# Attention plus gated MLP on one core: one q/k block transpose moved behind the next block's PV work, sums put in another order

## The chip, the core and the metric

One Trainium2 chip, one of its cores. The engines of a core run side by side, each through its own queue of instructions in order: TensorE (PE, matrix products; PEld is its weight load), VectorE (DVE), ScalarE (ACT), GpSimd (POOL) and SyncE (SP, which here only issues DMA transfers). The metric is device time in microseconds (us) for one launch of the whole kernel; less is better.

## The reference

Inputs are q, k, v of shape (8, 8, 576, 64) and the weights of an MLP. Attention is computed in separate chunks of 64 positions; its output, as 4608 rows of 512, goes through two matrix products with a swish between them.

```python
q_c = q.reshape(B, H, nc, chunk, D)            # k_c, v_c likewise, chunk = 64
scores = scale * np.matmul(q_c, k_c.transpose(0, 1, 2, 4, 3))
attn = np.exp(scores - np.max(scores, axis=-1, keepdims=True))
attn = attn / (np.sum(attn, axis=-1, keepdims=True) + 1e-09)
attn_out = np.matmul(attn, v_c)
...
x = attn_out.transpose(0, 2, 1, 3).reshape(B * S, H * D)   # 4608 x 512
h = x @ w_in                                               # 512 -> 2048
g = h * (1.0 / (1.0 + np.exp(-beta * h)))
return (g @ w_out).astype(np.float32)                      # 2048 -> 512
```

## The kernel before

The 4608 rows are nine blocks of 512 (`j` = 0 to 8, `NB` = 9). The order of all instructions is written out by hand: each engine runs its own in the order in which the Python code emits them. All matrix work is in fp16 with fp32 accumulation.

The loop over `j` = 1 to 8 (L675) works on two blocks at once: the MLP of block `j`, and, inside it, the attention of block `na = j + 1`, so that its input is there when the next turn begins.

**First product, `L1(j)` (L560).** x times w_in, partly by a seven-product (Strassen-Winograd) scheme: two `unit` calls make the hidden columns m = 0 to 7, and the plain products m = 8 to 15 (`emit_m`) stand between the unit's steps as spacers. A unit begins with the product `wA` on PE, which VectorE copies out of PSUM (`snap("u1")`, L319); the next product into the same bank (`wA<-xs,sw`) waits for this copy and for `xs`, the differences of x that `emit_xs` (L291 to L294) makes on VectorE. A unit has one sum on POOL (`t`, L342). `hooks` maps a number m to work that is emitted just ahead of `emit_m(j, m)`: loads of q, k, v, and block transposes. Block 1 alone goes through `L1_plain` (L540): there the first `nh` columns m are done in two halves of 256 rows, first halves first, since the last quarter of x still has to pass through a TensorE transpose (`emit_xp(7)`, in the hook -1) and a ScalarE copy (L235).

**Block transposes.** q and k of a batch arrive by DMA (`load_qk`, POOL queue); `T(b)` takes the next of batch b's four STREAM_TRANSPOSE instructions on VectorE (`emit_T`, L136; two halves of the heads, q and k each). Before the change `L1(j)` has all four of batch `j + 2` at the hooks 10, 13, 14 and 15. For `j` of 6 and more there is no batch `j + 2` left, and the hooks are empty.

**Sums.** The second product, g times w_out, uses the same seven-product scheme, and its operands are sums s1 to s4 of parts of g (`emit_sum(j, which, part)`, L373 for s3, L369 for s1, L371 for s2, L375 for s4), each in four parts p. Parts 0 and 2 of s3 are done on POOL, right after the units; all others on VectorE. s2 needs s1 of its part. The eight s1 and s2 sums are put on a list `fill` in the order p = 0, 2, 1, 3, and `dve(n)` emits the next n of them.

**Second product, `steps_L2(j)`.** Seven steps mm[0] to mm[6] on PE of 16 matmuls of 256 columns each. After mm[0], mm[2] and mm[4] ScalarE copies a bank out (u1, u2, u3, L422). After mm[2], POOL subtracts u1 and u2 (`w1`, printed as w, L449). `cB`, `cD` and `cC` are additions on VectorE (L430) whose results are stored, or kept as `t`.

**Attention of the next block.** `emit_sc` makes scores on PE and exponentials on ScalarE; `emit_pv(i, where)` makes 128 rows of x: 16 small matmuls into the PSUM bank `x` (where = "x") or into the two banks `sc0`, `sc1` (where = "s"), then on VectorE reciprocals (L210, L213) and products (L215), then a transposing DMA on SP's queue (L223) into `xt`. `pvs(n)` is the pair `emit_pv` n ("x") and n + 1 ("s"); the two pairs of a block, `pvs(0)` and `pvs(2)`, use the same banks, so PE can begin the second pair only when VectorE has read the first. `emit_xs(na)` waits for the four transposing DMAs.

So VectorE's order around the change is, for `j` from 2: unit 1, the hooks 13, 14, 15, s3 of parts 1 and 3, s1 and s2 of part 0 (`dve(2)`), `pvs(0)`, six sums (`dve(6)`), `pvs(2)`, four s4, cB, cD, xs, cC (`t`), and then the first copy (`u`) of the next unit.

Of the kernel before, what the change touches and what calls it, by code (L numbers as in the profile page):

```python
# [15 lines left out]
def kernel(  # L16
# [11 lines left out]
    B, H, S, D = q.shape  # L28
# [55 lines left out]
    def load_qk(b, split=False):  # L84
        for dst, nm in ((q_t, "qu"), (k_t, "ku")):
            dst[b] = qk_p.tile([128, 2, RUN, D], FP16, tag=nm, name=nm)
        for zs in ((slice(0, 1), slice(1, 2)) if split else (slice(0, 2),)):
            for src, dst in ((q, q_t), (k, k_t)):
                nc.gpsimd.dma_start(
                    out=dst[b][:, zs].rearrange("p z r d -> p z (r d)"),  # L90
                    in_=src[b].rearrange("(z a) (t r) d -> (a t) z (r d)", z=2, r=RUN)[:, zs],
                )
# [261 lines left out]
    def emit_m(j, m):  # L354
        emit_h(j, m)
        emit_g(j, m)
# [4 lines left out]
    def emit_sum(j, which, part):  # L361
        if j not in s_t:
            s_t[j] = [s_p.tile([128, NM, HT], FP16, tag=f"s{i}", name=f"s{i}") for i in range(4)]
        s1, s2, s3, s4 = s_t[j]
        g = gt_t[j]
        lo, hi = slice(2 * part, 2 * part + 2), slice(NM + 2 * part, NM + 2 * part + 2)
        tt = (nc.gpsimd if which == 3 and part in (0, 2) else nc.vector).tensor_tensor
        if which == 1:
            tt(out=s1[:, lo], in0=g[:, lo, dn], in1=g[:, hi, dn], op=ALU.add)  # L369
        elif which == 2:  # L370
            tt(out=s2[:, lo], in0=s1[:, lo], in1=g[:, lo, up], op=ALU.subtract)  # L371
        elif which == 3:
            tt(out=s3[:, lo], in0=g[:, lo, up], in1=g[:, lo, dn], op=ALU.subtract)  # L373
        else:
            tt(out=s4[:, lo], in0=g[:, hi, up], in1=s2[:, lo], op=ALU.subtract)  # L375
# [157 lines left out]
    fill = []  # L533

    def dve(n=1):
        for _ in range(n):
            if fill:
                fill.pop(0)()
# [21 lines left out]
    def L1(j, hooks={}, first=None):  # L560
        gt_t[j] = gt_p.tile([128, KFF, BLK], FP16, tag="gt", name="gt")

        def sp(m):
            def f():
                hooks.get(m, lambda: None)()
                emit_m(j, m)
            return f

        if first:
            first()  # L570
        unit(j, 0, [sp(8), sp(9), sp(10)])
        unit(j, 1, [sp(11), sp(12), sp(13)])
        for p in (0, 2):
            emit_sum(j, 3, p)
        sp(14)()
        sp(15)()
        for p in (0, 2, 1, 3):
            fill.extend([lambda w=w, p=p: emit_sum(j, w, p) for w in (1, 2)])
        hooks.get(KFF, lambda: None)()

    def table(func):
# [2 lines left out]
    with tc.manual_schedule():  # L584
        load_qk(0, split=True)
        nc.vector.memset(zero, 0.0)
        nc.vector.memset(bstage, 0.0)
        nc.vector.memset(warm, 0.0)
        nc.scalar.activation(out=warm2, in_=warm, func=ACTF.Exp, scale=1.0)
        for g4 in range(4):  # L590
            nc.sync.dma_start(
                out=bstage[32 * g4:32 * g4 + NM].rearrange("p r i -> p (r i)"),
                in_=moe_beta.rearrange("(m g x) -> g m x", g=4, x=64)[g4],
            )
        for t in vbuf:
            nc.vector.memset(t[:, :, :, D:D + 1], 1.0)
        load_v(0)
        make_identity(nc, ident)
        for g in range(4):
            load_w_in(g)  # L600
        load_w_out(0)
        load_w_out(1)
        load_qk(1)
        load_w_out(2)
        load_v(1)
        load_w_out(3)
        load_qk(2)

        emit_idle(4)
        for f in T_items(0):  # L610
            f()
        nc.vector.transpose(
            out=bt, in_=bstage.rearrange("p r i -> p (r i)").rearrange("p (i r) -> p r i", r=2)
        )
        eps = 2.0 ** -10
        nc.vector.tensor_tensor(out=bm, in0=bt, in1=bt, op=ALU.mult)
        nc.vector.tensor_scalar(
            out=bm, in0=bm, scalar1=eps * eps, scalar2=None, op0=ALU.is_ge)
        nc.vector.scalar_tensor_tensor(
            out=beta2, in0=bt, scalar=eps, in1=bm, op0=ALU.subtract, op1=ALU.mult)  # L620
        nc.vector.tensor_scalar_add(beta2, beta2, eps)
        nc.vector.reciprocal(out=binv, in_=beta2)
        emit_sc(0, between=lambda: emit_idle(5))
        emit_sc(1, where="p")
        emit_idle(3)
        emit_pv(0, xbar=False)
        emit_pv(1, where="p", xbar=False)
        d = emit_idle(4, 256)
        emit_xp(0)
        emit_pv(2, xbar=False)  # L630
        emit_idle(2, d=d)
        emit_xp(1)
        emit_pv(3, where="p", xbar=False)
        emit_idle(3, d=d)

        L1_plain(0, {-2: lambda: emit_xp(2), -3: lambda: emit_xp(3)}, 4)
        emit_sw()
        scale_w_out(0)
        scale_w_out(1)
        emit_tw(1)  # L640
        T1 = T_items(1)
        T1[0]()
        T1[1]()
        T1[2]()
        T1[3]()
        scale_w_out(2, act=2)
        table(ACTF.Exp)
        load_v(2)
        load_qk(3)
        hooks = {  # L650
            8: lambda: [emit_sc(2, "x"), emit_sc(3)],
            10: lambda: [emit_pv(4, xbar=False), emit_pv(5, "s", xbar=False), scale_w_out(3, act=2)],
            12: lambda: [emit_pv(6, xbar=False), emit_xp(4), emit_xp(5)],
            14: lambda: [emit_pv(7, xbar=False), emit_xp(6)],
        }
        for kk, f in enumerate(L2_plain(0)):
            hooks.get(kk, lambda: None)()
            f()

        TQ = {b: T_items(b) for b in range(2, B)}  # L660

        def T(b, n=1):
            for _ in range(n):
                if TQ.get(b):
                    TQ[b].pop(0)()

        def loads(j):
            if j + 3 < B:
                load_qk(j + 3)

        def loads_v(j):
            if j + 2 < B:
                load_v(j + 2)

        for j in range(1, NB):  # L675
            na = j + 1
            late = j == 1
            if late:
                L1_plain(1, {
                    -1: lambda: [emit_xp(7), table(ACTF.Silu)], 3: lambda: emit_tw(3), 4: lambda: T(2), 5: lambda: T(2),  # L680
                    6: lambda: emit_tw(2), 7: lambda: T(2), 9: lambda: T(2),
                    10: lambda: emit_tw(4), 14: lambda: T(3), 15: lambda: T(3),
                    11: lambda: [loads(1), loads_v(1)],
                    KFF: lambda: [table(ACTF.Exp), emit_sc(4, "x"), emit_sc(5)],
                }, 2)
            else:
                L1(j, {8: lambda: loads(j), 10: lambda: T(j + 2), 11: lambda: loads_v(j),
                       13: lambda: T(j + 2), 14: lambda: T(j + 2), 15: lambda: T(j + 2)})

            def pv(n, where):  # L690
                if na < NB:
                    emit_pv(4 * na + n, where)

            mm, cB, cD, cC = steps_L2(j, last=(j == NB - 1))
            def pvs(n):
                pv(n, "x")
                pv(n + 1, "s")

            mm[0]()
            emit_sum(j, 3, 1)  # L700
            emit_sum(j, 3, 3)
            if late:
                dve(8)
                T(3, 2)
            else:
                dve(2)
                pvs(0)
            mm[1]()
            if late:
                pvs(0)  # L710
            dve(6)
            mm[2]()
            if not late:
                pvs(2)
            if na + 1 < NB and not late:
                table(ACTF.Exp)
            mm[3]()
            if late:
                pvs(2)
            for p in (0, 2, 1, 3):  # L720
                emit_sum(j, 4, p)
            cB()
            mm[4]()
            cD()
            if na + 1 < NB:
                emit_sc(2 * na + 2, "x")
                emit_sc(2 * na + 3)
            if na < NB:
                emit_xs(na)
            mm[5]()  # L730
            if j < NB - 1:
                cC()
            mm[6]()
            if na + 1 < NB:
                table(ACTF.Silu)
# [30 lines left out]
```

## Time and profile before

| what | value |
|---|---|
| device time, median of 4 runs | 279.87 us (279.78 to 280.16) |
| device time of the profiled execution | 280.9 us |
| its span, first to last instruction | 279.1 us |
| mean granted TensorE clock | 1.000 |
| PE busy | 263.2 us, 94% of the span |
| VectorE busy | 211.9 us, 76% |
| ScalarE busy | 163.5 us, 59% |
| POOL busy | 100.9 us, 36% |

The loop's turns in this execution, by the start of the first product of the next block on PE: j = 1 from about 51 us, then 81, 109.4, 138.1, 166.9, 195.3, 222.6 and 248.9 us. In a line of the timeline the first number is the start in us from the span's start, the second the length of the (merged) group, then engine, source line, operation, written tile <- read tiles, shape, count; what stands in brackets is idle time of the engine before it and what ended it. A VectorE instruction that does not wait can begin some 80 ns before the recorded end of the one in front.

### The profile page before, as it was taken

The page shows a single profiled execution, that of the slowest core. Times are in us where ns is not written, and L with a number is a line of the kernel's source. Part 1 is how long each engine was busy: PE and PEld are TensorE (multiplying, and loading weights), DVE is VectorE, ACT ScalarE, POOL GpSimd, SP SyncE. Part 2 cuts the span into 40 slices and gives each one's busy share as a digit, 9 for nine tenths or more (in the row PEclk, how much of TensorE's full clock was granted, in tenths as well). Part 3 has the DMA queues.
Part 4 walks back from the last instruction along what each step waited for, and adds up shares of the span by engine and source line. Part 5 has one row for each costly group of instructions (what it writes and reads, how often), then busy time and mean ns, then how long its engine had stood idle before and what let it go on. Part 6 is the DMA issues. An engine that isn't in the chain of part 4 may idle for free.

```text
span 279.1 us, 8198 instructions
## 1 busy us (share of the span) xinstructions
PE 263.2 (94%) x3509; PEld 188.2 (67%) x3509; DVE 211.9 (76%) x425; ACT 163.5 (59%) x276; POOL 100.9 (36%) x108
## 2 busy tenths in 40 slices
PE   2689999999999999999989999999999999998995
PEld 0355455547876687668866886688668866876684
DVE  2762755879668997899789978898759766977674
ACT  2149746879166836684568546853785478225820
POOL 8732343190108610871078104820342035203500
PEclk9999999999999999999999999999999999999999
DMA  6999999999677926792669442914201420241013
GB/s 100 175 207 210 211 181 207 218 231 186 77 141 139 155 41 137 137 172 42 115 136 178 57 101 92 86 41 109 83 0 40 117 75 0 41 138 53 2 38 114
DMA packets 69588, 31.99 MB, mean 115 GB/s; under 512 B 53680, under 2 KB 63920, under 8 KB 69552
## 3 DMA queue, kind: packets, MB, share of 16 engines
q0 software_dynamic: 44960, 18.35, 54.5%
q1 hardware_dynamic: 24448, 12.99, 18.5%
q8 instruction: 27, 0.44, 0.7%
q10 hardware_dynamic: 144, 0.13, 0.1%
q14 instruction: 9, 0.07, 0.1%
HBM read 36.71 MB, written 9.44 MB: 165 GB/s over the span
## 4 chain that ended last, share of the span: by engine, by line
PE 65%; DVE 19%; DMA 9%; issue 2%; ACT 2%; POOL 2%; DVEq 0%; ACTq 0%; POOLq 0%
PE hps L258 22%; PE oA L411 11%; PE wA L311 8%; DMA xt<-x 6%; PE wX L311 5%; PE ops L510 5%; DVE x L215 4%; PE oD L411 3%; PE oB L411 3%; DMA vb<-in_v_dram 3%; DVE s L371 3%; PE oC L411 2%; DVE kT L136 2%; DVE u L319 2%; DVE s L369 1%
## 5 line engine op out<-in xcount | busy, mean ns | idle before, releaser
L258 PE MATMUL hps<-xt,wi 128*128 128x512 f16 (+1 forms) x376 | 85.3, 365 | 0.6 <-ACT xt L235 0.5
L268 ACT ACTIVATE gt<-hps,beta 128x512 f16<-128x512 f32 x88 | 57.5, 681 | 24.3 <-PE hps L258 24.3
L258 PEld LDWEIGHTS <-wi 128*128 128x128 f16 x376 | 36.7, 98 | 29.7 <-issue 1.1
L411 PEld LDWEIGHTS <-s 128*128 128x128 f16 x496 | 47.8, 98 | 5.9 <-DVE s L375 0.2
L411 PE MATMUL oA<-tw,s 128*128 128x256 f16 x368 | 44.0, 273 | 0.0
L411 PEld LDWEIGHTS <-gt 128*128 128x128 f16 x384 | 36.0, 98 | 6.8 <-issue 0.2
L422 ACT COPY u<-oA 128x512 f32<-128x512 f32 x24 | 14.0, 585 | 41.5 <-PE oA L411 41.5
L99 POOL DMA_DIRECT2D vb<-in_v_dram x32 | 27.4, 876 | 10.4 <-DMA wi<-in_moe_w_in_dram 6.2
L311 PEld LDWEIGHTS <-sw 128*128 128x128 f16 x224 | 21.9, 98 | 13.1 <-issue 4.6
L480 POOL TENSOR_TENSOR o<-t,o 128x512 f32<-128x512 f32 x7 | 8.9, 1271 | 58.1 <-issue 35.3
L342 POOL TENSOR_TENSOR t<-u,w 128x512 f32<-128x512 f32 x14 | 17.9, 1275 | 32.2 <-DVE u L319 32.2
L319 DVE COPY u<-wA 128x512 f32<-128x512 f32 x42 | 28.6, 680 | 0.9 <-PE wA L311 0.9
L449 POOL TENSOR_TENSOR w<-u,u 128x512 f32<-128x512 f32 x7 | 9.4, 1339 | 41.6 <-ACT u L422 30.9
L136 DVE STREAM_TRANSPOSE qT<-qu 128x576 f32<-128x576 f32 x16 | 19.9, 1244 | 5.1 <-DMA qu<-in_q_dram 5.1
L136 DVE STREAM_TRANSPOSE kT<-ku 128x576 f32<-128x576 f32 x16 | 19.9, 1244 | 4.2 <-DMA ku<-in_k_dram 4.2
L373 POOL TENSOR_TENSOR s<-gt 128x512 f16<-128x512 f16 x16 | 19.2, 1220 | 8.9 <-ACT gt L268 8.9
L311 PE MATMUL wA<-xs,sw 128*128 128x256 f16 x112 | 16.8, 272 | 3.7 <-DVE u L319 3.7
L311 PEld LDWEIGHTS <-wi 128*128 128x128 f16 x168 | 16.4, 98 | 4.9
L322 ACT ACTIVATE gt<-c,beta 128x512 f16<-128x512 f32 x28 | 18.7, 716 | 0.3
L168 PEld LDWEIGHTS <-kT 32*64 32x64 f16 x1152 | 11.6, 109 | 10.4 <-DVE kT L136 6.7
L371 DVE TENSOR_TENSOR s<-s,gt 128x512 f16<-128x512 f16 x32 | 17.5, 546 | 1.1
L582 ACT ACT_TABLE_LOAD x14 | 18.0, 1283 | 0.2
(87 smaller groups left out, 400.4 us busy)
## 6 DMA issues: line engine op xcount, KB each, us to landing
out_dram<-osb SPq DMA_DIRECT2D x21, 256.0 KB, 2.6
vb<-in_v_dram POOLq DMA_DIRECT2D x32, 144.0 KB, 8.0
qu<-in_q_dram POOLq DMA_DIRECT2D x7, 576.0 KB, 7.9
ku<-in_k_dram POOLq DMA_DIRECT2D x7, 576.0 KB, 10.1
out_dram<-o SPq DMA_DIRECT2D x14, 256.0 KB, 2.2
wi<-in_moe_w_in_dram POOLq DMA_DIRECT2D x4, 512.0 KB, 12.4
w_out<-in_moe_w_out_dram POOLq DMA_DIRECT2D x4, 512.0 KB, 16.8
qu<-in_q_dram POOLq DMA_DIRECT2D x2, 288.0 KB, 5.5
```

The lines of the kernel that those rows point to most:

```text
L99: nc.gpsimd.dma_start(out=t[64 * hp:64 * hp + 64, 2 * z:2 * z + 2, :, 0:D].rearrange("p s c d -> p (s c) d"), in_=v[b, h0:h0 + 2].rearrang ...
L136: nc.vector.transpose(out=dst[b][:, z].rearrange("p t r e -> p (t r e)").bitcast(FP32).rearrange("p (t r) -> p r t", r=RUN), in_=src[b][:, ...
L258: nc.tensor.matmul(out=hps_t[j, m][:, c0:c1], lhsT=w_r[m // 4][:, 2 * z + e, m // 2 % 2, m % 2, :], rhs=xt_t[j][:, n, c0:c1], start=(n == ...
L268: nc.scalar.activation(out=gt_t[j][:, m, :], in_=hps, func=ACTF.Silu, scale=beta2[:, m % 2, m // 2:m // 2 + 1],)
L311: nc.tensor.matmul(out=bank[b][:, i, :], lhsT=a[:, kk, q, i, :], rhs=rhs[:, kk, :], start=(first and i == 0 and kk == 0), stop=(kk == 1), ...
L319: nc.vector.tensor_copy(out=sb[nm], in_=bank[b])
L322: nc.scalar.activation(out=gt_t[j][:, m, cols], in_=src, func=ACTF.Silu, scale=beta2[:, m % 2, m // 2:m // 2 + 1],)
L342: nc.gpsimd.tensor_tensor(out=sb["t"], in0=sb["u3"], in1=sb["w1"], op=ALU.add)
L371: tt(out=s2[:, lo], in0=s1[:, lo], in1=g[:, lo, up], op=ALU.subtract)
L373: tt(out=s3[:, lo], in0=g[:, lo, up], in1=g[:, lo, dn], op=ALU.subtract)
L411: nc.tensor.matmul(out=bank[name][:, i, :], lhsT=a[:, kk, i * 128:(i + 1) * 128], rhs=b[:, kk, :], start=(first and i == 0 and n == 0), st ...
L582: nc.scalar.activation(out=warm2, in_=warm, func=func, scale=1.0)
```

## The change

Six edits, all in the order in which work is emitted; no operation is added to or taken from VectorE, ScalarE, POOL or SP.

1. Block 1: the number `nh` of columns m done in halves goes from 2 to 3.
2. For `j` = 2 to 5 the hook 15 is emptied: `L1(j)` has three transposes of batch `j + 2`, at the hooks 10, 13, 14. The fourth (the first in the batch's order) is emitted one turn earlier, by a `T(j + 3)` ahead of `emit_xs(na)`; for that `j` runs from 1 to 4.
3. `fill` gets its eight sums ahead of `sp(14)` and `sp(15)`.
4. For `j` = 2 to 5, `dve(2)` (s1 and s2 of part 0) stands ahead of the two s3 sums on VectorE.
5. For `j` = 6, 7, 8 (`light`, no batch `j + 2`), the hooks 14 and 15 have `dve(2)` each: s1 and s2 of the parts 0 and 2.
6. For these `j`, `dve(2)` and `pvs(2)` stand ahead of the rest of the sums and of mm[2]; before, mm[2] was ahead of `pvs(2)`. Block 8 has no next block, so there `pvs` does nothing.

```diff
@@ L1
         for p in (0, 2):
             emit_sum(j, 3, p)
+        for p in (0, 2, 1, 3):
+            fill.extend([lambda w=w, p=p: emit_sum(j, w, p) for w in (1, 2)])
         sp(14)()
         sp(15)()
-        for p in (0, 2, 1, 3):
-            fill.extend([lambda w=w, p=p: emit_sum(j, w, p) for w in (1, 2)])
         hooks.get(KFF, lambda: None)()
@@ the loop over j
-                }, 2)
+                }, 3)
             else:
                 L1(j, {8: lambda: loads(j), 10: lambda: T(j + 2), 11: lambda: loads_v(j),
-                       13: lambda: T(j + 2), 14: lambda: T(j + 2), 15: lambda: T(j + 2)})
+                       13: lambda: T(j + 2), 14: lambda: T(j + 2) if j + 2 < B else dve(2),
+                       15: lambda: dve(2) if j + 2 >= B else None})
...
+            light = j + 2 >= B
             mm[0]()
+            if not late and not light:
+                dve(2)
             emit_sum(j, 3, 1)
             emit_sum(j, 3, 3)
             if late:
                 dve(8)
                 T(3, 2)
             else:
-                dve(2)
                 pvs(0)
             mm[1]()
             if late:
                 pvs(0)
+            if light:
+                dve(2)
+                pvs(2)
             dve(6)
             mm[2]()
-            if not late:
+            if not late and not light:
                 pvs(2)
...
             if na + 1 < NB:
                 emit_sc(2 * na + 2, "x")
                 emit_sc(2 * na + 3)
+            T(j + 3)
             if na < NB:
                 emit_xs(na)
```

## The prediction

> **What bounds the kernel now.** I read, in this order, the chain of waits, the list of who waited for whom, and the timelines of single engines around the places that the change touches.
>
> ```profile
> PE 65%; DVE 19%; DMA 9%; issue 2%; ACT 2%; POOL 2%; DVEq 0%; ACTq 0%; POOLq 0%
> ```
>
> ```profile
> PE wA L311 <- DVE u L319: 3.7, 5, 1.1
> ```
>
> The chain is PE for 65%, and PE is busy for 263.2 of 279.1 us. A reordering can win only where PE stands still. After the start-up, PE's idle time is five waits of 3.7 us in all, each at the second `wA` product of a block, plus one stall in block 1. The timeline has the five at 83.57 (0.62 us), 112.28 (0.89), 140.86 (0.75), 169.13 (0.44) and 251.94 (1.05). There is none at the starts of blocks 6 and 7.
>
> What is late there is VectorE. Its timeline in block 2:
>
> ```profile
> 95.19 1.23 DVE L136 STREAM_TRANSPOSE kT<-ku 128x576 f32<-128x576 f32 x1
> 96.28 0.73 DVE L373 TENSOR_TENSOR s<-gt 128x512 f16<-128x512 f16 x2
> ...
> 97.71 0.20 DVE L213 RECIPROCAL rd<-x 128x8 f32<-128x8 f32 x1
> ...
> 101.23 0.42 DVE L369 TENSOR_TENSOR s<-gt 128x512 f16<-128x512 f16 x1
> 101.68 1.44 DVE L371 TENSOR_TENSOR s<-s,gt 128x512 f16<-128x512 f16 x1
> 103.05 0.19 DVE L213 RECIPROCAL rd<-x 128x8 f32<-128x8 f32 x1
> ...
> 109.47 0.43 DVE L291 TENSOR_TENSOR xs<-xt 128x512 f16<-128x512 f16 x1 [1.87 <-DMA xt<-x]
> ```
>
> The second reciprocal group (103.05) starts `pvs(2)`; 6.42 us later its x has been transposed by DMA and xs begins; 2.81 us after that PE gets its copy `u` and goes on at 112.28. So each us by which 103.05 comes earlier takes up to a us from the stall. Ahead of it stands an s2 sum of 1.44 us, where the others take 0.42. POOL's timeline tells why, first in block 2, then in block 6:
>
> ```profile
> 93.92 2.27 POOL L373 TENSOR_TENSOR s<-gt 128x512 f16<-128x512 f16 x2
> 101.58 1.26 POOL L449 TENSOR_TENSOR w<-u,u 128x512 f32<-128x512 f32 x1 [5.38 <-ACT u L422]
> ```
>
> ```profile
> 206.06 1.27 POOL L342 TENSOR_TENSOR t<-u,w 128x512 f32<-128x512 f32 x1 [4.47 <-DVE u L319]
> 207.29 2.27 POOL L373 TENSOR_TENSOR s<-gt 128x512 f16<-128x512 f16 x2
> 214.88 1.53 POOL L449 TENSOR_TENSOR w<-u,u 128x512 f32<-128x512 f32 x1 [5.33 <-DVE s L369]
> ```
>
> The sum began at 101.68, POOL's w at 101.58; the sum ended at 103.12, 0.28 us after w (102.84). Blocks 3, 4 and 5 show the same 0.28 (131.76 against 131.48, 160.36 against 160.08, 188.62 against 188.34). In block 6 the sum began at 214.86, 0.02 us ahead of w: it took its usual 0.42, and w took 1.53 instead of 1.26. A VectorE sum of two SBUF operands and a POOL operation thus exclude each other, the first goes first, and a sum that comes second ends 0.28 us after POOL's. Transposes and operations with a PSUM operand are not held: the transpose at 95.19 ran at its usual 1.23 us beside POOL's s3.
>
> **Part 1, block 1 (`nh` 3).** The timeline of PE:
>
> ```profile
> 51.08 0.60 PE L258 MATMUL hps<-xt,wi 128*128 128x256 f16 x4
> 51.92 2.33 PE L258 MATMUL hps<-xt,wi 128*128 128x256 f16 x14 [0.24 <-ACT xt L235]
> ```
>
> Matmuls of 256 columns start every 0.109 us. The four at 51.08 would be followed at 51.52; the next starts at 51.92, so 0.40 us are lost to the ScalarE copy of x. Four more first-half matmuls (4 x 0.109 = 0.44) fill just that. They need a third bank of L1, freed by the copy at 49.76 to 50.35. Work is the same: two matmuls of 0.109 for one of 0.217. Gain 0.39. It stays: in block 1 the `pvs(2)` reciprocal waits for PE (74.19, idle 1.94), so VectorE's chain moves along. Bounds 0 and 0.40.
>
> **Part 2, the moved transpose (blocks 1 to 4).** It adds nothing and issues no DMA. At its new place VectorE is idle for 2.02, 1.87, 1.82 and 1.50 us (the brackets at xs); it costs there 1.07 to 1.09 us (start to next start). Its q data are long there (the load issued at 58.3 lands after 7.3 us; in later blocks it is issued over 20 us ahead). Queued behind it is xs, which waits for the DMA anyway: price 0. Without this cover, that is if the DMA landed over 0.4 to 0.9 us earlier and cB and cD did not, it would cost what is missing, at most 1.09 a block; but cB and cD move with the chain (below).
>
> **Part 3, blocks 2 to 5.** The transpose at 95.19 goes, and s1, s2 of part 0 come ahead of s3. This does not free 1.1 us, since the first sum now arrives at 95.19 while POOL's second s3 runs from 95.03 to E = 96.19. It is held and ends at E + 0.283. Then, by the pitches of the trace (dependent sum 0.035 after the end, then 0.342, 0.335, 0.33): s2 at E + 0.318, s3 at E + 0.660 and E + 0.995, reciprocal at E + 1.325 = 97.52 instead of 97.71. A mere 0.2 us. But the six sums follow: from that reciprocal to the last s2 the trace has 3.97 us, so this s2 starts at E + 5.30, and w starts at E + 5.385, 5.329, 5.320, 5.315 (blocks 2 to 5). The sum now leads by 84, 28, 19 and 14 ns where it was 100 to 170 behind. In blocks 6 and 7 of this trace the same four sums already follow a held one, and the last leads w by 20 ns in both: it goes first. I take it that it does so here. Then the second reciprocal starts at 97.52 + 3.97 + 0.34 = 101.83 instead of 103.05, 1.22 us earlier. The PE data are there (PE wrote x until 101.1), and s4, cB, cD move by as much: cD is done by about 106.3 (u3, copied at 104.77 to 105.36, is in time), the transpose by 107.4, the DMA at 109.47 - 1.22 = 108.25. PE then could go on at 111.06, and it is ready at 112.28 - 0.89 = 111.39: no stall. Blocks 3 and 4 the same way. Gains 0.89 + 0.75 + 0.44 = 2.08; the start of block 6 has no stall to lose. POOL's w is 0.27 later, and is needed (cC) only 6 us on. Bounds: 0 if w goes first, 2.08.
>
> **Part 4, blocks 6 to 8.** Here the sums enter POOL's busiest stretch: t to 207.34, s3 to 208.45 and 209.56. VectorE is free at 206.88. Each wait as above, and POOL held as in 214.88 (its operation ends 1.12 or, for s3, 1.02 after the sum's end): s1 ends 207.62; POOL's first s3, which came in between, ends 208.63; s2, queued behind, ends 208.92; POOL's second s3 ends 209.94; s1 of part 2 ends 210.22; s2, s3, s3, and the reciprocal at 211.26, against 210.89 before. Now mm[2] no longer stands between the pairs: PE is at its second x bank at 212.21 and at the sc banks at 212.38, and VectorE has read the second one only 2.02 us after the reciprocal, at 213.28, plus 0.05 for the signal. PE stalls 213.33 - 212.38 = 0.95 us. Bounds: 0.14 if no sum is held (the reciprocal then waits for PE's x at 210.4), and 1.36 if POOL keeps the port through its three queued operations (s1 ends 209.84, reciprocal 211.67, bank 213.74). Nearest row: every held instruction of the trace waited for one instruction of the other engine, so I take 0.95. Block 6 had no stall at its end: +0.95. Block 7 had 1.05, and its x now comes more than 1 us earlier: 0.95 - 1.05 = -0.10. Block 8 has no second pair, and its s3 (done near 266.3) is used at 266.75: 0. Sum +0.85.
>
> The Trainium skill, "SBUF — State Buffer", section "Who interferes with whom", has the exclusive lock and says that issue order decides who blocks. By it the sum, waiting since 206.88, goes ahead of POOL's s3 of 207.29, which would make the total of all parts -1.62; if POOL's queue were served through, it would be -0.80. Its summary, "Schedule whichever is off the critical path", speaks against these hooks. No run here shows both engines queued.
>
> **Sum.** -0.39 - 2.08 + 0.85 = -1.62 on the span of 279.1. The profiled execution (280.9) and the median (279.87) have the same work around the span, so I carry it to the median: 279.87 - 1.62 = 278.25, say 278.3. A change within 0.2% (0.56 us: 279.31 to 280.43) could not be told from none.
>
> **Rivals.**
> POOL keeps the port through its queue, but the close leads hold: two stalls of 1.36, so 2.72 - 1.05 = +1.67 instead of +0.85; 279.87 - 0.39 - 2.08 + 1.67 = 279.1. For it: t, s3, s3 follow with starts before the previous end (207.29 before 207.34). Against: no held row is longer than one operation.
> Slower: POOL has precedence, at every close meeting. Place: the last s2 of blocks 2 to 5, where a lead of 14 to 84 ns no longer counts, and the queue of blocks 6 and 7. Price: the 2.08 is gone and the light blocks cost 1.67; 279.87 - 0.39 + 1.67 = 281.15. It decides if a lead of more than 84 ns is needed. For it: the leads are my arithmetic, good to some 20 ns. Against: 20 ns sufficed twice.
> The change does only a part of what it could: the lead suffices in block 2 (84 ns), not in 3 to 5. 279.87 - 0.39 - 0.89 + 0.85 = 279.4, no change that can be told.
> No sum is held in the hooks: stalls of 0.14, 0.28 - 1.05 = -0.77, and 276.6. Against: t and w are the same kind of operation, and w held a sum four times.
>
> **How the numbers follow.** Forecast 0.44, POOL's queue 0.22, precedence 0.12, block 2 alone 0.10, nothing held 0.05, anything unseen 0.07, which I count as slower. Faster: 0.41 of the forecast (it lies 1.1 us past the bound), 0.16 of the queue case (only 0.2 past it), 0.05: 0.62. Same: 0.03 + 0.06 + 0.09 = 0.18. Slower: 0.12 + 0.07 + 0.01 = 0.20. The range 277.4 to 280.1 holds the forecast with an error of 0.8 below, the queue case and block 2 alone; it leaves out precedence, nothing held and a part of the unseen.
>
> **What would show it.** Right: PE's wait for `u` only at 83.57 and gone at the starts of blocks 3, 4, 5 and 8; the last s2 of blocks 2 to 5 at 0.42 us, with w at 1.5; the first sum of blocks 2 to 5 held to 0.28 after POOL's s3; PE idle 0.9 before `xp` of the second pair in blocks 6 and 7; no idle at `hps` near 51.9. Wrong: an s2 still of 1.4 us, a POOL s3 pair of the usual 2.27 beside the sums of block 6, or xs waiting for the moved transpose instead of the DMA.

## The result, and the profile after

| | before | after |
|---|---|---|
| device time, median | 280.13 us (63 runs) | 278.94 us (39 runs) |
| ratio after / before, 95% interval | | 0.9958 [0.9946, 0.9971] |
| span of the profiled execution | 279.1 us | 277.6 us |
| PE busy, share of the span | 94% | 95% |

The runs of before are those made beside the runs of after; the ratio is 1.2 us less (0.8 to 1.5). The forecast was 1.6 us less.

The page of the kernel after: the busy time of each engine, and the chain that ended last.

```profile
PE 263.6 (95%) x3513; PEld 188.9 (68%) x3513; DVE 217.7 (78%) x425; ACT 163.5 (59%) x276; POOL 102.5 (37%) x108
...
PE 85%; DVE 7%; DMA 3%; POOL 2%; issue 1%; ACT 1%; DVEq 0%; ACTq 0%; POOLq 0%
```

PE's share of the chain rises from 65% to 85%: most of the places where the chain left PE for VectorE and a DMA are gone. VectorE's busy time has grown by 5.8 us with the same 425 instructions. It is held more often, which costs nothing where PE does not wait for it.

PE's list of waits after (us in total, times, the longest):

```profile
PE xp L198 <- DVE x L215: 1.0, 4, 0.3
...
PE oA L411 <- issue: 0.4, 1, 0.4
PE wA L311 <- DVE u L319: 0.4, 1, 0.4
```

The five waits for `u` (3.7 us) have become one. Two entries are new: PE waits four times at `xp`, and once for nothing that the profile shows ("issue"). Where the time went is best read from the length of each block on PE, taken from the starts of the first `wA` product of each block (block 1 from the first of its `hps`, block 8 to the end of the span):

| us | start to first hps | block 0 | block 1 | 2 to 5 | 6 | 7 | 8 | 6 to 8 |
|---|---|---|---|---|---|---|---|---|
| before | 18.45 | 31.97 | 30.64 | 114.15 | 27.52 | 26.26 | 30.13 | 83.91 |
| after | 18.79 | 31.93 | 30.76 | 111.43 | 28.55 | 27.25 | 28.89 | 84.69 |
| difference | +0.34 | -0.04 | +0.12 | -2.72 | +1.03 | +0.99 | -1.24 | +0.78 |
| forecast | 0 | 0 | -0.39 | -2.08 | +0.95 | +0.95 | -1.05 | +0.85 |

The start-up's +0.34 lies ahead of everything that was edited: the v load of batch 0 landed later (PE waited 0.86 us for it instead of 0.41). So it is no effect of the change; it varies from run to run: the eleven kernels of the experiments have their first `hps` anywhere from 17.6 to 18.7.

**Blocks 2 to 5.** VectorE's timeline after, in block 2, then POOL's:

```profile
95.40 1.27 DVE L369 TENSOR_TENSOR s<-gt 128x512 f16<-128x512 f16 x1
96.71 0.43 DVE L371 TENSOR_TENSOR s<-s,gt 128x512 f16<-128x512 f16 x1
97.05 0.75 DVE L373 TENSOR_TENSOR s<-gt 128x512 f16<-128x512 f16 x2
97.72 0.20 DVE L213 RECIPROCAL rd<-x 128x8 f32<-128x8 f32 x1
...
101.70 0.42 DVE L371 TENSOR_TENSOR s<-s,gt 128x512 f16<-128x512 f16 x1
102.04 0.20 DVE L213 RECIPROCAL rd<-x 128x8 f32<-128x8 f32 x1
...
106.51 1.25 DVE L136 STREAM_TRANSPOSE qT<-qu 128x576 f32<-128x576 f32 x1
108.50 0.43 DVE L291 TENSOR_TENSOR xs<-xt 128x512 f16<-128x512 f16 x1 [0.74 <-DMA xt<-x]
```

```profile
94.12 2.27 POOL L373 TENSOR_TENSOR s<-gt 128x512 f16<-128x512 f16 x2
101.78 1.47 POOL L449 TENSOR_TENSOR w<-u,u 128x512 f32<-128x512 f32 x1 [5.39 <-DVE s L369]
```

POOL's second s3 ends at 94.12 + 2.27 = 96.39. The first sum is held until 0.28 us after that (95.40 + 1.27 = 96.67). The last s2 starts at 101.70, the end of s3 plus 5.31, some 80 ns ahead of w. It takes 0.42 us, and now w is the longer one (1.47 instead of 1.26). In blocks 2 to 5 the leads were 86, 37, 17 and 25 ns. The moved transpose at 106.51 stands where VectorE still waits for the DMA afterwards (0.74 us at `xs`).

**Blocks 6 and 7.** VectorE, POOL and PE in block 6 of the kernel after:

```profile
204.57 0.74 DVE L369 TENSOR_TENSOR s<-gt 128x512 f16<-128x512 f16 x1
205.35 1.26 DVE L371 TENSOR_TENSOR s<-s,gt 128x512 f16<-128x512 f16 x1
206.53 1.37 DVE L369 TENSOR_TENSOR s<-gt 128x512 f16<-128x512 f16 x1
207.94 0.43 DVE L371 TENSOR_TENSOR s<-s,gt 128x512 f16<-128x512 f16 x1
...
208.95 0.20 DVE L213 RECIPROCAL rd<-x 128x8 f32<-128x8 f32 x1
```

```profile
203.76 1.27 POOL L342 TENSOR_TENSOR t<-u,w 128x512 f32<-128x512 f32 x1 [4.47 <-DVE u L319]
204.99 2.63 POOL L373 TENSOR_TENSOR s<-gt 128x512 f16<-128x512 f16 x2
```

```profile
210.48 0.21 PE L198 MATMUL xp<-vb,et 64*64 64x65 f16 x1 [0.16 <-DVE x L215]
211.03 0.32 PE L198 MATMUL xp<-vb,et 64*64 64x65 f16 x15 [0.33 <-DVE x L215]
```

Three sums in a row are held (0.74, 1.26, 1.37 us), and POOL's s3 pair takes 2.63 instead of 2.27: the two engines take turns, one instruction each. PE then stands at the second pair's banks, once for the first half and once for the second.

### The profile page after: what moved, and what is told of

It is laid out like the page before. It is cut to its first block, busy times and chain, and to the rows that moved or that the text cites. A ratio compares the mean times of both kernels' runs of the same rounds, so it can differ in the third digit from the quotient of the medians.

```text
span 277.6 us, 8206 instructions
## 1 busy us (share of the span) xinstructions
PE 263.6 (95%) x3513; PEld 188.9 (68%) x3513; DVE 217.7 (78%) x425; ACT 163.5 (59%) x276; POOL 102.5 (37%) x108
## 3 DMA queue, kind: packets, MB, share of 16 engines
q1 hardware_dynamic: 24448, 12.99, 17.6%
## 4 chain that ended last, share of the span: by engine, by line
PE 85%; DVE 7%; DMA 3%; POOL 2%; issue 1%; ACT 1%; DVEq 0%; ACTq 0%; POOLq 0%
PE hps L258 25%; PE oA L411 19%; PE wA L311 9%; PE wX L311 6%; PE oD L411 5%; PE ops L510 5%; PE oC L411 5%; PE oB L411 4%; DMA vb<-in_v_dram 3%; PE sc L168 2%; PE scx L168 2%; DVE s L369 1%; DVE x L215 1%; PE x L198 1%; DVE s L371 1%
## 5 line engine op out<-in xcount | busy, mean ns | idle before, releaser
L373 POOL TENSOR_TENSOR s<-gt 128x512 f16<-128x512 f16 x16 | 20.2, 1282 | 9.9 <-ACT gt L268 9.9
L369 DVE TENSOR_TENSOR s<-gt 128x512 f16<-128x512 f16 x32 | 20.6, 644 | 0.0
L371 DVE TENSOR_TENSOR s<-s,gt 128x512 f16<-128x512 f16 x32 | 18.1, 566 | 1.1
L322 ACT ACTIVATE gt<-c,beta 128x512 f16<-128x512 f32 x28 | 18.7, 716 | 0.3
```

Source lines behind the costliest of these rows:

```text
L322: nc.scalar.activation(out=gt_t[j][:, m, cols], in_=src, func=ACTF.Silu, scale=beta2[:, m % 2, m // 2:m // 2 + 1],)
```

## The experiments

Blocks are timed as in the table above. Ratios are to the kernel before. e3, e10 and e11 have one more source line ahead, so their line numbers are higher by one.

| us | 1 | 2 to 5 | 6 to 8 | median | ratio to before, 95% |
|---|---|---|---|---|---|
| after | 30.76 | 111.43 | 84.69 | 278.94 | 0.9958 [0.9946, 0.9971] |
| e1_nh2 | 30.77 | 111.08 | 84.70 | 278.55 | 0.9943 [0.9922, 0.9964] |
| e2_vlate | 30.18 | 115.81 | 84.83 | 282.48 | 1.0077 [1.0046, 1.0108] |
| e3_delay | 31.09 | 113.83 | 84.78 | 280.70 | 1.0012 [0.9995, 1.0029] |
| e4_mm2first | 30.83 | 111.98 | 83.78 | 278.53 | 0.9936 [0.9915, 0.9957] |
| e5_T_alone | 30.91 | 111.78 | 84.35 | 278.23 | 0.9916 [0.9881, 0.9950] |
| e6_hooks | 30.64 | 111.32 | 82.77 | 277.26 | 0.9883 [0.9836, 0.9931] |
| e7_v_first | 30.03 | 111.84 | 84.70 | 279.04 | 0.9952 [0.9925, 0.9979] |
| e8_pairs | 31.09 | 111.63 | 86.29 | 280.52 | 1.0026 [0.9999, 1.0052] |
| e9_best | 30.03 | 111.50 | 82.74 | 276.74 | 0.9871 [0.9827, 0.9914] |
| e10_delay_small | 30.80 | 111.49 | 84.70 | 278.95 | 0.9949 [0.9922, 0.9977] |
| e11_delay_mid | 30.61 | 112.29 | 84.90 | 280.12 | 0.9994 [0.9976, 1.0013] |

### Block 1: what became of the closed stall

**e1_nh2**: the kernel after with `nh` back at 2.

```diff
-                }, 3)
+                }, 2)
```

> The changed kernel with two columns in halves in block 1 again (part 1 undone). Theory (TensorE's instructions from number 1730 on come at about 72.2 us whatever it does before, in both profiles): the stall of 0.24 at hps near 51.9 is back, the one near 72.2 (0.40, released by nothing that the profile shows) is gone or below 0.1, and the start of block 2 stays within 0.15 us of the changed kernel's 81.48, so that part 1 is worth nothing there; time within 0.1%. Rival (the stall at 72.2 is an accident of one execution): block 2 starts 0.4 us later than in a run with part 1, and the time is 0.4 us longer.

The stall at `hps` is back (0.24 us at 51.54) and the "issue" stall is no longer listed; block 1 takes 30.77 us instead of 30.76. The matmul at 72 us is still 0.19 us late, more than was expected (the table below has its step of 0.30). Edit 1 is worth nothing as it stands: what it saves at 51 us is waited for at 72. Block 1 takes 30.64 to 30.91 us in the three profiles with `nh` 2 (before, e1_nh2, e5_T_alone) and 30.61 to 31.09 in the seven with `nh` 3 and the v load in its place. The lines of PE's timeline of the kernel after, around 51 us and around 72 us:

```profile
51.38 3.86 PE L258 MATMUL hps<-xt,wi 128*128 128x256 f16 x27
```

```profile
70.06 1.70 PE L411 MATMUL oA<-tw,s 128*128 128x256 f16 x14
72.17 0.39 PE L411 MATMUL oA<-tw,s 128*128 128x256 f16 x2 [0.40 <-issue]
```

There is no wait at `hps` any more. But PE stops after the fourteenth of sixteen like matmuls. No operand sets this. Counted in the trace's records of PE's stream, it is the 864th matmul, and the 864th is the one that is late in each kernel that loads v behind q and k, whatever it computes (with `nh` 2 four matmuls fewer come before it, so there it is the third of `oD`). Starts in us; undisturbed, the step is 0.109. The last two columns are read from the trace's DMA records: the last end, before the 864th matmul, of a 16 KB packet of the instruction queue (q8), and the time from there to the 864th:

| | 863rd matmul | 864th | step | packet ends | to the 864th |
|---|---|---|---|---|---|
| before (`oD`) | 72.02 | 72.17 | 0.16 | 70.74 | 1.43 |
| after (`oA`) | 71.49 | 72.17 | 0.68 | 70.78 | 1.39 |
| e1_nh2 (`oD`) | 71.64 | 71.94 | 0.30 | 70.71 | 1.23 |
| e5_T_alone (`oD`) | 72.28 | 72.72 | 0.44 | 71.26 | 1.46 |
| e2_vlate (`oA`), v load moved | 70.69 | 70.80 | 0.11 | 67.04 | 3.75 |
| e7_v_first (`oA`), v load moved | 71.74 | 71.85 | 0.11 | 70.36 | 1.49 |

A place in the stream that is late for whatever stands there suggests that the instructions themselves come late, and the packet bears this out. In the ten profiles where it is late, the 864th matmul begins anywhere from 71.15 to 72.72 us, but always 1.23 to 1.46 us after that packet's end. In the kernel after the packet starts at 69.82 us, among the packets of the v load, which run on q0 until about 72.

**e2_vlate** and **e7_v_first** therefore move that v load: to the end of the block, or ahead of the q and k loads.

```diff
# e2_vlate
-                    11: lambda: [loads(1), loads_v(1)],
+                    11: lambda: loads(1),
...
+            if late:
+                loads_v(1)
             T(j + 3)
# e7_v_first
-                    11: lambda: [loads(1), loads_v(1)],
+                    11: lambda: [loads_v(1), loads(1)],
```

> The changed kernel with the load of v for batch 3 moved in block 1 from the hook 11 to just ahead of the moved transpose. Theory (the load of TensorE's instructions stands behind the v packets of 66 to 72 us): the stall at 72.2 is gone, block 2 starts 0.4 to 0.55 us earlier (near 80.9 if the start-up is as late as in the changed kernel's profile). Rival (the stall has to do with the place in the code, not with the DMA traffic): still 0.40 near 72.2, and block 2 at 81.5.

> The changed kernel with the two loads of the hook 11 of block 1 exchanged: v of batch 3 ahead of q and k of batch 4. Theory (the TensorE instructions from number 1729 on come late because their load stands behind the v packets of 66 to 72 us, 256 bytes each): with the v packets earlier and q, k (4.6 KB rows) in their place the instruction load comes earlier, no stall near 72, block 1 of 30.2 us instead of 30.76, and the gain of part 1 stays; the moved transpose still finds its q at 79. Rival (any load in that place delays it): the stall stays within 0.15 us of 0.40.

PE's timeline of e7_v_first at the same place:

```profile
70.31 1.92 PE L411 MATMUL oA<-tw,s 128*128 128x256 f16 x16
72.06 1.15 PE L411 MATMUL oD<-tw,gt 128*128 128x256 f16 x9
```

All sixteen run on, and so they do in e2_vlate, where the packet of q8 starts at 66.1 us. Block 1 becomes 0.73 and 0.58 us shorter than after. The stall thus hangs on where the v load stands. In e7_v_first the packet, now among those of q and k, starts at 69.4 us, 18.4 us after the block's first `hps` instead of 18.8 to 19.3 in the seven kernels with `nh` 3 and v behind: it is just in time. That the instruction load queues behind the packets of these loads is the reading that fits; the queueing itself is in no record.

Neither gains its time at the end. In e7_v_first the stall at the start of block 2 grows from 0.40 to 0.79 us: blocks 1 and 2 together take 58.64 instead of 58.98, and the timing shows no difference from the kernel after. For e2_vlate only the gain in block 1 was expected, and not what the move does to block 2. Its waits on PE:

```profile
PE hps L258 <- DMA xt<-x: 3.3, 1, 3.3
PE wA L311 <- DVE u L319: 1.3, 1, 1.3
```

The v packets now run beside the DMAs that transpose x for block 2; PE waits 4.6 us for their data, and the block is 4.4 us longer.

### Blocks 2 to 5: who goes first, and what brings it about

**e5_T_alone**: the kernel before with the moved transpose only (edits 1 and 3 to 6 left out).

```diff
-                       13: lambda: T(j + 2), 14: lambda: T(j + 2), 15: lambda: T(j + 2)})
+                       13: lambda: T(j + 2), 14: lambda: T(j + 2)})
...
+            T(j + 3)
             if na < NB:
                 emit_xs(na)
```

> The kernel before with the moved transpose alone (part 2 of the prediction; the sums stay behind s3, no other edit). Theory (the four sums start held by POOL's second s3 in either order and end at the same 1.33 us after it, so the new order of part 3 is worth nothing and the moved transpose alone wins the race of the last s2 with w): the last s2 of blocks 2 to 5 leads w by 10 to 90 ns and takes 0.42; no stall at the starts of blocks 3, 4, 5; blocks 3, 4, 5 as long as in the changed kernel (27.6 to 27.9 us); blocks 6, 7, 8 as before (27.5, 26.3, 30.1); time about 2.5 us under the kernel before. Rival (the order of the sums is needed): s2 of 1.4 us and the old stalls.

Blocks 2 to 5 take 111.78 us, 2.37 less than before, against 2.72 with the whole change. The last s2 led w by 58, 3, 4 and 1 ns, and went first each time. Block 4 (4 ns), VectorE and POOL:

```profile
157.62 0.42 DVE L371 TENSOR_TENSOR s<-s,gt 128x512 f16<-128x512 f16 x1
```

```profile
157.63 1.55 POOL L449 TENSOR_TENSOR w<-u,u 128x512 f32<-128x512 f32 x1 [5.33 <-DVE s L369]
```

So the new order of the sums (edit 4) is not what gains; in these two profiles the leads with it are 13 to 34 ns longer. Timed, the moved transpose alone is 0.8% under the kernel before (0.5 to 1.2), at least as much as the whole change.

**e3_delay, e10_delay_small, e11_delay_mid**: the kernel after with a memset on VectorE behind `dve(2)` in blocks 2 to 5, of 256, 64 and 128 columns, so that the six sums come later and nothing else changes.

```diff
+    pause = const.tile([128, 256], FP32)
...
             if not late and not light:
                 dve(2)
+                nc.vector.memset(pause, 0.0)
```

> The changed kernel with one memset of 128x256 on VectorE, about 0.24 us, between the sums of part 0 and the s3 sums of blocks 2 to 5; its result is not used. Theory (the gain of these blocks hangs on the last s2 leading POOL's w by 17 to 86 ns): the sum now comes 0.15 to 0.22 us after w, is held (1.2 to 1.4 us), the stalls at the starts of blocks 3, 4, 5 come back with about 0.9, 0.75, 0.45 us of idle and the time rises by 2 to 2.6 us. Rival (the gain is VectorE's time saved by the moved transpose, 1.1 us a block): 0.24 us are hidden, sums of 0.42, no stall, time unchanged.

> The changed kernel with a memset of 128x64 instead of 128x256 on VectorE at the same place in blocks 2 to 5 (about 0.06 us). Theory (who starts first gets the port): the lead of block 2 (0.07 to 0.09 us) shrinks to about 0.02 and the sum still goes first; the leads of blocks 3, 4, 5 (0.012 to 0.037 us) turn into 0.02 to 0.05 us behind, these sums are held for 1.3 us, and the stalls of blocks 4 and 5 come back (0.75 and 0.4 us of idle), not that of block 3; time 1.3 to 1.6 us over the changed kernel. Rival (a sum is held only when it comes 0.1 us or more behind): all four keep 0.42 us, time unchanged.

> The changed kernel with a memset of 128x128 at the place of the two delay runs. The memset of 64 columns moved the leads by some 20 ns, that of 256 by 220; this one should move them by about 85 to 110: block 2 to about -20 to 0 ns, blocks 3, 4, 5 to -50 to -90. Theory (who starts first gets the port): the three sums of blocks 3, 4, 5 are held (1.3 to 1.4 us), and stalls of about 0.8 and 0.4 us of idle come back at the starts of blocks 4 and 5 (none at block 6), 0.9 at the start of block 3 if block 2 is behind too; time 1.3 to 2.5 us over the changed kernel. Rival (only 0.1 us or more behind counts): 0.42 us each and no stall.

With 256 columns the last s2 is 132 to 189 ns behind w in all four blocks. It takes 1.37 to 1.42 us again, and the stalls at the starts of blocks 3, 4 and 5 are back with 1.02, 0.82 and 0.10 us. Blocks 2 to 5 lose 2.40 us of the 2.72. Timed, it is 1.5 us over the kernel after, less than was expected of it. With the 64 columns the leads were only 7 to 29 ns shorter than in the kernel after: 64, 8, 9 and 18 ns, all won, and a time like that of the kernel after (278.95 us, 0.9949 [0.9922, 0.9977]). That delay was chosen too short to tell anything more. With 128 columns the lead was 12 ns in block 2 (won, 0.43 us) and -49, -50 and -47 ns in the blocks 3 to 5, all lost. Block 3 of e11_delay_mid, VectorE and POOL:

```profile
128.85 1.49 DVE L372 TENSOR_TENSOR s<-s,gt 128x512 f16<-128x512 f16 x1
```

```profile
128.80 1.26 POOL L450 TENSOR_TENSOR w<-u,u 128x512 f32<-128x512 f32 x1 [5.33 <-ACT u L423]
```

Between 1 ns ahead and 47 ns behind, the same sum goes from 0.42 to 1.5 us, and w from 1.55 to 1.26: the earlier start decides. Not each lost sum became a stall, though. Block 4 of e11_delay_mid began with one of 0.50 us, block 5 with none, and timed it is 1.0 us over the kernel after, where 1.3 to 2.5 was expected. Where `xs` waited for the last transposing DMA, it began 3.0 to 4.7 us after that DMA's issue in these traces (8.5 in block 1 of e2_vlate, beside the v packets). An early landing leaves less of a late sum over at the end: ahead of block 5 of e11_delay_mid `xs` began 3.3 us after the issue, without waiting.

### Blocks 6 to 8: which of the two light edits costs

**e4_mm2first** has mm[2] ahead of `pvs(2)` again, and the other sums behind it; **e6_hooks** has edit 5 without edit 6; **e8_pairs** has edit 6 without edit 5.

```diff
# e4_mm2first
             if light:
                 dve(2)
-                pvs(2)
-            dve(6)
+            else:
+                dve(6)
             mm[2]()
-            if not late and not light:
+            if not late:
                 pvs(2)
+            dve(6)
# e6_hooks
-            if light:
-                dve(2)
-                pvs(2)
             dve(6)
             mm[2]()
-            if not late and not light:
+            if not late:
                 pvs(2)
# e8_pairs
-                       13: lambda: T(j + 2), 14: lambda: T(j + 2) if j + 2 < B else dve(2),
-                       15: lambda: dve(2) if j + 2 >= B else None})
+                       13: lambda: T(j + 2), 14: lambda: T(j + 2),
+                       15: lambda: None})
```

> The changed kernel with mm[2] ahead of pvs(2) again in blocks 6 and 7, but the sums of part 3 behind pvs(2). Theory (the 0.95 us in each of these blocks is TensorE waiting for VectorE to read the sc banks of the first pair): no idle at xp, block 6 shorter by 1.0 us, block 7 by 1.0 with at most 0.2 us of stall at the start of block 8, since the second pair's reciprocal starts about 0.9 us earlier than in the kernel before; time 1.8 to 2.0 us less than the changed kernel. Rival (the pair order is what removes the stall of block 8): block 7 shorter, but 0.8 us or more of stall come back at the start of block 8, time 1.0 us less.

> The changed kernel with mm[2] ahead of pvs(2) in blocks 6 to 8, but the sums still in the hooks 14 and 15 (edit 5 without edit 6). Theory: sums and POOL's operations take turns in the hooks as in the changed kernel, the first reciprocal of blocks 6 and 7 starts about 0.37 us later than before, but TensorE does not stall at xp; the second reciprocal starts about 0.45 us earlier than before, so block 6 has its old 27.5 us, block 7 its old 26.3, and the stall at the start of block 8 is 0.5 to 0.7 us of idle instead of 1.05; time 1.3 to 1.6 us under the changed kernel. Rival (the hooks cost the time, not the order): blocks 6 and 7 stay near 28.5 and 27.2.

> The changed kernel with the hooks 14 and 15 empty in blocks 6 to 8, but pvs(2) ahead of mm[2] (edit 6 without edit 5; dve(2) ahead of pvs(2) then takes part 0). Theory: the first reciprocal waits only for TensorE's x, so the stall at xp falls from 0.95 to about 0.2 to 0.4 us; but six sums then come behind pvs(2), the last s2 is late for mm[4], and TensorE waits there for about 1 us in blocks 6 and 7; total within 0.7 us of the changed kernel. Rival (the stall at xp comes from the order alone): it stays at 0.9.

| us | block 6 | block 7 | block 8 |
|---|---|---|---|
| before | 27.52 | 26.26 | 30.13 |
| after | 28.55 | 27.25 | 28.89 |
| e4_mm2first | 27.99 | 26.69 | 29.10 |
| e6_hooks | 27.62 | 26.22 | 28.93 |
| e8_pairs | 29.34 | 28.04 | 28.91 |

All three lack the wait at `xp`, e4_mm2first and e6_hooks because mm[2] stands between the pairs again, e8_pairs because no sums in the hooks hold up the first pair (its reciprocal starts 15.24 us into block 6 instead of 16.04). In e4_mm2first half of what was expected is missing, and in e8_pairs blocks 6 to 8 came out 1.6 us longer than in the kernel after, where a difference of at most 0.7 was expected. The reason is the same line in both; PE's waits of e4_mm2first, then of e8_pairs:

```profile
PE oA L411 <- DVE s L371: 0.6, 2, 0.3
```

```profile
PE oA L411 <- DVE s L371: 2.4, 6, 0.4
```

Sums that come behind `pvs(2)` on VectorE are late for mm[4], the step that multiplies by them. In e8_pairs no sum is made in the hooks and only two stand ahead of `pvs(2)`; mm[4] waits three times for sums in each of blocks 6 and 7. In e6_hooks all are made in time; its waits on PE from block 1 on, all of them:

```profile
PE wA L311 <- DVE u L319: 0.4, 1, 0.4
...
PE oA L411 <- issue: 0.3, 1, 0.3
```

So edit 5 alone has what was good in the light blocks: block 7's end stall gone (-1.20 in block 8), and nothing lost in 6 and 7. Its block 8 came out better than expected. Part of that is seen at `xs` in block 7 of e6_hooks:

```profile
238.65 0.42 DVE L371 TENSOR_TENSOR s<-s,gt 128x512 f16<-128x512 f16 x1
238.99 0.20 DVE L213 RECIPROCAL rd<-x 128x8 f32<-128x8 f32 x1
...
244.60 0.43 DVE L291 TENSOR_TENSOR xs<-xt 128x512 f16<-128x512 f16 x1 [0.91 <-DMA xt<-x]
```

From the reciprocal to `xs` are 5.61 us, where block 7 of before had 6.41: `xs` began 3.37 us after the issue of the last transposing DMA, instead of 4.17. Why these landings differ stays open.

**e9_best**: e6_hooks and e7_v_first together.

> The changed kernel with mm[2] ahead of pvs(2) in blocks 6 to 8 (as in the run with the sums in the hooks and the old pair order) and with v ahead of q and k in the hook 11 of block 1. Theory: no stall near 72, none at xp; blocks 1 and 2 together 58.6 to 58.9 us, block 6 27.6, block 7 26.2, blocks 8 28.9 to 29.4; 1.0 to 1.2% under the kernel before. Rival (the short block 8 of the earlier run was an accident of its DMA landing): block 8 of 29.6 and more, 0.8%.

276.74 us, 1.3% less than before (3.6 us; interval 2.4 to 4.8), where the kernel after has 0.4% (0.3 to 0.5). The largest stall left behind the start-up is one of 0.50 us at the start of block 2. Block 8 takes 28.92 us (28.93 in e6_hooks); `xs` ahead of it again began early, 3.0 us after the last issue. Against e6_hooks alone (0.9883 [0.9836, 0.9931]) the timing shows no difference, so what stands as gained over the kernel after is undoing edit 6.

## Why the prediction was right, and where it was not

**Right in sign and near in size, by two errors that cancel in part.** Part 1 gave nothing, and part 3 gave more than forecast; that they met near the forecast is luck. The kernel became 1.2 us faster where 1.6 was forecast. In the profiled executions the parts sum to -1.82 (0.12 - 2.72 + 0.78) instead of -1.62, to which the start-up and block 0, not touched by the change, add 0.30.

**Part 1: wrong.** The step that failed is "It stays: in block 1 the `pvs(2)` reciprocal waits for PE (74.19, idle 1.94), so VectorE's chain moves along." The stall at `hps` did go, as worked out. But 20 us later PE waits at its 864th matmul, by the reading above for its instructions. Counted from the block's first `hps`, that matmul begins after 21.75 to 22.03 us in the three profiles with `nh` 2 and after 21.30 to 21.78 in the seven with `nh` 3. With `nh` 3 four more matmuls (0.44 us) stand ahead of it, so the work behind it is no earlier. That it starts at 72.17 both before and after is in part chance, since block 1 began 0.30 us later in the kernel after. e1_nh2 shows the worth as nothing, e2_vlate and e7_v_first show that block 1 does become shorter when the v load stands elsewhere. The profile of before held a faint hint: its 864th matmul began 0.05 us late, far too little to be listed as a wait. Even without this, e7_v_first shows that the x of block 2 would not have come as much earlier: its start then waits 0.79 us.

**Part 2: right.** The moved transpose cost nothing in the kernel after; `xs` still waited 0.63 to 0.89 us for the DMA behind it. Where the DMA landed early, as at the end of block 2 of e7_v_first, `xs` began right behind the transpose, 5.56 us after the reciprocal, and the next block began without a stall.

**Part 3: mechanism right, size too small.** The close meetings went as forecast (leads of 84, 28, 19, 14 ns forecast, 86, 37, 17, 25 measured). The term mis-sized is "Gains 0.89 + 0.75 + 0.44 = 2.08", which measured 1.09 + 0.91 + 0.51 = 2.51 by the lengths of blocks 3 to 5; another 0.21 came from block 2's own start (0.62 of idle became 0.40), which the forecast left as it was. The idle time that the profile lists understates a stall of PE. The start of block 3 after, where nothing is waited for:

```profile
111.00 0.60 PE L311 MATMUL wX<-xt,wi 128*128 128x256 f16 x4
111.44 0.60 PE L311 MATMUL wA<-xs,sw 128*128 128x256 f16 x4
```

The four at 111.00 are recorded as ending at 111.60, yet the next could begin at 111.44. Idle counts from the recorded end, so each listed stall is 0.16 us short: 1.05 + 0.91 + 0.60 = 2.56. What also was not seen is that the order of the sums, which the working needed for its leads, was not needed: e5_T_alone won in blocks 3 to 5 with 1 to 4 ns.

**Part 4: right.** With block 6 beginning 2.30 us earlier than before (192.91 against 195.21), the forecast second read of the bank and PE's going on at 213.33 become 211.03; PE goes on at 211.03. The forecast reciprocal at 211.26 becomes 208.96; it is at 208.95. The first sum's end, 207.62, becomes 205.32; 204.57 + 0.74 = 205.31. The waits listed are only 0.16 + 0.33 a block because a single matmul stands between them and for the reason just given; by the blocks' lengths they cost 1.03 and 0.99. Block 8's gain of 1.24 is about the 1.05 listed, with the 0.16 (1.21).

**Rivals.** POOL keeping the port through its queue is refuted by the held sums: 0.74 and 1.26, where the first would have taken until POOL's third operation ended. Precedence of POOL is refuted by every close meeting that VectorE won, down to 1 ns in e5_T_alone. That the lead would do in block 2 only is refuted by the 0.42 us of the last s2 in all four blocks. That no sum is held in the hooks is refuted by the held sums of block 6. Section "Who interferes with whom" of the Trainium skill's "SBUF — State Buffer" has an exclusive lock and says that issue order decides who blocks; the rows here agree, including those where both queues had more to do (s1 waiting, served ahead of POOL's s3).

## What to carry to other kernels

A gain at a stall is real only if what comes behind it moves too: look along the same engine for the next event that has its own clock, such as a transfer or the supply of instructions, and for hitches there that are too small to be listed. Where two engines exclude each other, as here, less than 50 ns can decide over a us, so a reordering pays when it changes who is first; work that can run in some later wait is best moved there from just ahead of such a meeting. Before work is taken out from between two users of the same buffer, count how long the first user's readers need: here mm[2] was the cover, and putting it back while keeping the early sums beat both kernels.

## What the runs showed of the hardware

- **PE stood at one fixed place of its instruction stream, whatever the work there.** Its 864th matmul was late by 0.05 to 0.90 us in all ten profiles with v loaded behind q and k, each time 1.23 to 1.46 us after the end of a 16 KB packet of the instruction queue, and on time in the three with the v load moved (1.49 us or more after it: e2_vlate, e7_v_first, e9_best). Late instructions are the reading that fits.
- **The exclusion of VectorE and POOL turns on less than 50 ns.** A sum that starts 1 ns ahead takes 0.42 us, one that starts 47 ns behind 1.5; nothing between was measured. Where both have a queue they take turns instruction by instruction (the s3 pair of 2.63 us).
- **Like transposing DMAs differ in how soon they land.** `xs`, where it waited for the last one, began 3.0 to 4.7 us after its issue; with the packets of a v load beside it, 8.5 us (e2_vlate).
